# A filler tile in SBUF: the K and V buffers of a decode kernel begin at multiples of 512 bytes

## The chip, the cores and the metric

The kernel runs on one core of a Trainium2 chip. The metric is device time in microseconds (us); the kernel before takes 670.23 us, the median of three runs (670.22 to 670.27). TensorE is PE in the profile, VectorE is DVE, ScalarE is ACT, GpSimd is POOL and SyncE is SP. DMA transfers are issued by SP, and at the start by ACT, and carried out by 16 DMA engines.

## The reference

One decode step of a transformer block for four tokens (B = 4, width 512). A conditioning vector gives six modulation vectors. The first half is attention of one query per batch over a cache of 4096 keys and values in each of 32 heads of 128 elements; the second half is a small gated MLP.

```python
mod = (_silu(c) @ w_mod).reshape(c.shape[0], 6, 1, -1)
h = _layernorm(x, axis=-1) * (1 + ca) + sa
x = x + ga * _A_ref(h, A_k_cache, A_v_cache, A_wq, A_wo)   # attention over the cache
h = _layernorm(x, axis=-1) * (1 + cb) + sb
x = x + gb * _B_ref(h, B_w_in, B_w_sp, B_b_sp, B_w_out)    # gated MLP
```

Inside `_A_ref`: `q = x @ wq`, scores `q . k` for 4096 keys, softmax, the weighted sum of the values, and the projection by `wo`. All inputs are bf16. The two caches hold 4 x 32 x 4096 x 128 elements each, 134 MB each; all else is small beside them.

## The kernel before, in words

**Tiling.** The 128 (batch, head) pairs are treated four heads at a time: NQ = 32 rounds, round i being head group g = i // 4 of batch b = i % 4. A round needs 4 MiB of K and 4 MiB of V. A K tile lies as [128 partitions, 128 x 128 elements]: partition 32 h + s holds the 128 consecutive keys of slot s of head h, 32,768 consecutive bytes of the cache. V lies the same way. So each partition of a tile is one unbroken piece in HBM and one in SBUF.

**Buffers.** Two K tiles (kt0, kt1) and two V tiles (vt0, vt1), each 32,768 bytes a partition, are the first tiles of the SBUF pool `sb`; the pool hands out places in the order in which tiles are asked for. In front of them lie 16,384 bytes that the program keeps for DMA and four small constants, so kt0 begins at byte 16512 of each partition. Behind them come some 80 small tiles: the identity `ident`, the query `qbc` (8192 bytes), softmax vectors, weights. Before round 0 the V tiles serve as landing places for two weights, w_mod in vt0 and wq in vt1.

**A round.** SP issues the load of the next K tile and of this round's V tile (line 141, where every DMA is recorded). In some rounds a 512 KB piece of `wo` (tile wo_g) is loaded too. DVE multiplies half a K tile by the query in place (`scores`, recorded at line 136: kt<-kt,qbc, 8192 elements), and PE adds up the 128 products of each key by 16 matmuls with the identity (lines 355 and 360). DVE folds the partial sums (S<-bank), does the softmax's maximum by reductions and transposes (mx, mT, hm, hb, nm), ACT takes the exponential (E), and DVE spreads it over the four heads (P). PE multiplies the V tile of the round before by P (line 349, bank<-vt,P), and ACT copies the result out (osb).

**What sets the order.** `Program` records every operation, finds which one needs which by the regions of the tiles that they read and write, and gives each engine its operations in the order of the Python code, with semaphore waits. A K load waits until PE has finished with the tile that it overwrites, a V load until PE has finished the values of two rounds before. SP issues in that fixed order.

**The end.** The last K and V tiles are loaded in pieces, and behind them on the same queue come the last part of wo (wo_l), win and wout. A tail of small operations (projection, layer norm, gated MLP) follows, and a transfer of 4 KB brings the output to HBM.

The functions that allocate, as the diff touches them:

```python
    def tile2(shape, dtype, name, n=2):
        return [sb.tile(shape, dtype, name=f"{name}{a}") for a in range(n)]

    kt = tile2([P, NT * DH], BF16, "kt")
    vt = tile2([P, NT * DH], BF16, "vt")
```

Of the kernel before, what the change touches and what calls it, by code (L numbers as in the profile page):

```python
# [7 lines left out]
BF16 = mybir.dt.bfloat16  # L8
# [218 lines left out]
def kernel(  # L227
# [17 lines left out]
    P = 128  # L245
# [19 lines left out]
    sb = ctx.enter_context(tc.tile_pool(name="sb", bufs=1))  # L265
    pm = ctx.enter_context(tc.tile_pool(name="pm", bufs=1, space=bass.MemoryType.PSUM))

    def tile2(shape, dtype, name, n=2):
        return [sb.tile(shape, dtype, name=f"{name}{a}") for a in range(n)]

    kt = tile2([P, NT * DH], BF16, "kt")
    vt = tile2([P, NT * DH], BF16, "vt")
    rows = sb.tile([2 * B, D], BF16, name="rows")
# [500 lines left out]
```

## Time and profile before

| what | value |
|---|---|
| median of three runs | 670.23 us (670.22 to 670.27) |
| the profiled execution | 670.11 us |
| its span, first to last instruction | 668.3 us |
| DVE busy | 402.9 us, 60% of the span, 475 instructions |
| PE busy | 420.4 us, 63% |
| ACT busy | 41.3 us, 6% |
| bytes by DMA | 282.90 MB in 12673 packets, mean 423 GB/s |
| granted TensorE clock, mean | 0.772 |

How to read the views. The slices cut the span in 40 equal parts, each digit being the busy share of an engine in tenths. A row of a group of instructions names line, engine, operation, output<-inputs with their shapes, the count, then busy time and the mean ns of one, then the idle time of the engine just before them and what ended it. A row of DMA issues gives the count, the KB of one and the median us from issue to landing. A row of the table by windows gives the window, its length, then for each engine the busy us and (in brackets) the instructions, in the order PE, PEld (weight loads), DVE, ACT, POOL, then the granted clock, the DMA share and GB/s. A timeline row gives start, length, engine, line and operation; in square brackets stands the idle time before it and what ended it. A packet is one descriptor's piece of a transfer on one DMA engine.

### The profile page before, as it was taken

To read this page: it belongs to the slowest core of one execution; us is meant where nothing else is said; L and a number is where in the kernel's file an instruction comes from. 1 tells how busy PE (TensorE), PEld (TensorE's weight loads), DVE (VectorE), ACT (ScalarE), POOL (GpSimd) and SP (SyncE) were. 2 spreads that over 40 slices of the span, in tenths; PEclk is the share of its full clock that TensorE was granted. 3 is DMA by queue.
4 is the path that set the end of the run, shared out by engine and by line. 5 is a ranking of instruction groups with operands and counts; after the bars stand their busy time and mean duration, and the time that the engine had idled before them with its cause. 6 is when DMAs were issued, how large, how long until landed. Compare 5 with 4: busy or idle time off the path is not lost.

```text
span 668.3 us, 5909 instructions
## 1 busy us (share of the span) xinstructions
PE 420.4 (63%) x3024; PEld 94.2 (14%) x2065; DVE 402.9 (60%) x475; ACT 41.3 (6%) x115; POOL 3.2 (0%) x17
## 2 busy tenths in 40 slices
PE   2557776665576754576655667656557675557784
PEld 2201110011111101111001111101111110111124
DVE  2177766676456666555756654757655666655662
ACT  1200000000000000000000000000000000000002
POOL 1000000000000000000000000000000000000000
PEclk9988876767888767888766788766788876788885
DMA  9999999999999999999999999999999999999995
GB/s 377 430 426 430 436 430 430 429 437 426 431 431 437 430 426 431 435 430 426 435 435 430 430 431 435 430 428 431 437 428 430 431 437 426 431 431 437 422 410 198
DMA packets 12673, 282.90 MB, mean 423 GB/s; under 512 B 1388, under 2 KB 1908, under 8 KB 3956
## 3 DMA queue, kind: packets, MB, share of 16 engines
q1 hardware_dynamic: 12640, 282.73, 98.8%
q8 instruction: 7, 0.11, 0.1%
q14 instruction: 6, 0.05, 0.0%
q10 hardware_dynamic: 20, 0.01, 0.0%
HBM read 282.73 MB, written 0.00 MB: 423 GB/s over the span
## 4 chain that ended last, share of the span: by engine, by line
DMA 63%; PE 24%; DVE 12%; issue 0%; SPq 0%; ACT 0%; DVEq 0%
DMA kt<-in_A_k_cache_dram 58%; PE bank L360 23%; DVE kt L136 11%; DMA vt<-in_A_v_cache_dram 3%; DMA wout<-in_B_w_out_dram 1%; PE bank L349 0%; SPq L141 0%; DVE S L136 0%; DVE P L136 0%; ACT E L136 0%; DVE mx L136 0%; DVE nm L136 0%; DVE mT L136 0%; DVE hm L136 0%; DVE hb L136 0%
## 5 line engine op out<-in xcount | busy, mean ns | idle before, releaser
L360 PE MATMUL bank<-kt,ident 128*128 128x512 bf16 x1024 | 295.0, 459 | 180.9 <-DVE kt L136 180.9
L136 DVE TENSOR_TENSOR kt<-kt,qbc 128x8192 bf16<-128x8192 bf16 x64 | 282.7, 4420 | 86.6 <-DMA kt<-in_A_k_cache_dram 86.6
L136 DVE TENSOR_REDUCE S<-bank 128x64 f32<-128x512 f32 x64 | 44.3, 692 | 125.6 <-PE bank L360 125.6
L355 PEld LDWEIGHTS <-ident 128*128 128x128 bf16 x64 | 9.1, 142 | 359.4 <-issue 359.3
L349 PE MATMUL bank<-vt,P 128*32 128x512 bf16 x992 | 59.2, 380 | 0.5 <-DMA vt<-in_A_v_cache_dram 0.5
L349 PE MATMUL bank<-sel,osb 128*128 128x4 f32 x248 | 35.7, 267 | 29.4 <-ACT osb L136 25.0
L136 ACT ACTIVATE E<-S,nm 128x128 f32<-128x128 f32 x32 | 12.8, 401 | 568.3 <-DVE nm L136 568.3
L349 PEld LDWEIGHTS bank<-sel,osb 128*128 128x128 f32 x248 | 33.0, 207 | 41.9 <-ACT osb L136 36.9
L136 DVE TENSOR_TENSOR P<-E,mask 128x512 bf16<-128x512 f32 x32 | 22.2, 693 | 18.0 <-ACT E L136 18.0
L349 PEld LDWEIGHTS bank<-rs,ones_f 128*128 128x128 f32 x64 | 12.1, 190 | 104.8 <-issue 104.0
L349 PEld LDWEIGHTS bank<-vt,P 128*32 128x32 bf16 x992 | 23.6, 96 | 21.4 <-DMA vt<-in_A_v_cache_dram 0.6
L136 ACT COPY osb<-bank 128x512 f32<-128x512 f32 x31 | 17.5, 565 | 17.4 <-PE bank L349 17.3
L349 PE MATMUL bank<-vt,hbc 128*32 128x512 bf16 x128 | 8.9, 448 | 4.7 <-DMA vt<-in_A_wq_dram 4.7
L349 PE MATMUL bank<-oP,wo_g 128*128 128x4 bf16 x112 | 3.9, 165 | 10.2 <-DVE oP L136 10.2
L136 DVE RECIPROCAL rz<-bank 128x4 f32<-128x4 f32 x32 | 5.6, 176 | 7.3 <-PE bank L349 7.3
L136 DVE TENSOR_REDUCE mx<-S 128x1 f32<-128x128 f32 x32 | 9.2, 286 | 1.1
L349 PE MATMUL bank<-rs,ones_f 128*128 128x4 f32 x64 | 9.1, 212 | 0.0
L136 DVE STREAM_TRANSPOSE nm<-hb 128x32 f32<-128x32 f32 x32 | 6.8, 212 | 1.1
L136 DVE STREAM_TRANSPOSE mT<-mx 128x32 f32<-128x32 f32 x32 | 6.8, 212 | 1.1
L136 DVE TENSOR_SCALAR rs<-mask,rs 128x4 f32<-128x4 f32 x32 | 7.2, 224 | 0.0
L136 DVE TENSOR_REDUCE hm<-mT 128x1 f32<-128x32 f32 x32 | 6.0, 186 | 1.1
L136 DVE TENSOR_SCALAR hb<-hm 128x32 f32<-128x32 f32 x32 | 5.8, 181 | 1.1
(91 smaller groups left out, 75.5 us busy)
## 6 DMA issues: line engine op xcount, KB each, us to landing
kt<-in_A_k_cache_dram SPq DMA_DIRECT2D x31, 4096.0 KB, 25.8
vt<-in_A_v_cache_dram SPq DMA_DIRECT2D x31, 4096.0 KB, 33.1
vt<-in_A_wq_dram SPq DMA_DIRECT2D x1, 4096.0 KB, 20.5
kt<-in_A_k_cache_dram SPq DMA_DIRECT2D x2, 2048.0 KB, 24.7
wo_g<-in_A_wo_dram SPq DMA_DIRECT2D x7, 512.0 KB, 22.8
vt<-in_w_mod_dram SPq DMA_DIRECT2D x1, 3072.0 KB, 10.2
vt<-in_A_v_cache_dram SPq DMA_DIRECT2D x1, 2048.0 KB, 19.8
win<-in_B_w_in_dram SPq DMA_DIRECT2D x1, 1344.0 KB, 14.8
```

What stands on the lines that cost most here:

```text
L136: eng, lambda e: getattr(e, name)(*args, **kw), ins, outs, sem=sem, done=done, after=after,
L349: "PE", lambda e: e.matmul(out, lhsT=lhsT, rhs=rhs, start=start, stop=stop, **kw),
L355: prog.add("PE", lambda e: e.ldweights(lhsT), [lhsT], [], done=False)
L360: return e.add_instruction(mybir.InstMatmult(name=nc.get_next_instruction_name(), engine=mybir.EngineType.PE, ins=[e.lower_ap(rhs), e.lowe ...
```

## The change

One tile is asked for ahead of kt0, 192 bf16 elements (384 bytes) on each partition. Nothing reads or writes it. The tiles after it keep their order and sizes.

```diff
@@ -268,6 +268,8 @@
     def tile2(shape, dtype, name, n=2):
         return [sb.tile(shape, dtype, name=f"{name}{a}") for a in range(n)]
 
+
+    fill = sb.tile([P, 192], BF16, name="fill")
     kt = tile2([P, NT * DH], BF16, "kt")
     vt = tile2([P, NT * DH], BF16, "vt")
     rows = sb.tile([2 * B, D], BF16, name="rows")
```

## The prediction

> **What bounds the kernel now.** I read the page's slices first. The three rows are the busy share of DVE, the mean busy share of the 16 DMA engines, and the rate.
>
> ```profile
> DVE  2177766676456666555756654757655666655662
> ...
> DMA  9999999999999999999999999999999999999995
> GB/s 377 430 426 430 436 430 430 429 437 426 431 431 437 430 426 431 435 430 426 435 435 430 430 431 435 430 428 431 437 428 430 431 437 426 431 431 437 422 410 198
> ```
>
> The DMA digit is 9 up to the last slice, while DVE is near 6. The rate is flat at about 431 GB/s, so the stream of K and V has no hole. The DMA part of the page names the queue that carries it, with its packets, megabytes and share of 16 engines' span:
>
> ```profile
> q1 hardware_dynamic: 12640, 282.73, 98.8%
> ```
>
> Next the table by windows, cut at 40 us (loop running), 620, 650 and 663 us (last landing; I leave out the windows between). Its last two numbers are DMA share and GB/s.
>
> ```profile
> 2.00:10.00 8.00, 0.50 (x9) 0.44 (x9) 0.96 (x6) 1.47 (x2) 1.90 (x10) 1.00 1.01 399
> ...
> 40.00:620.00 580.00, 368.04 (x2394) 73.15 (x1502) 365.36 (x396) 28.45 (x89) 0.00 (x0) 0.76 1.00 431
> ...
> 650.00:663.00 13.00, 8.50 (x220) 7.81 (x220) 2.72 (x17) 2.87 (x6) 0.00 (x0) 0.51 0.80 302
> 663.00:668.30 5.30, 0.91 (x19) 0.54 (x16) 1.40 (x8) 1.11 (x3) 0.22 (x1) 0.50 0.00 1
> ```
>
> The share is 1.00 while K and V stream, 0.80 while the last weights come, and 0 after 663. The timeline of the end shows what starts the tail:
>
> ```profile
> 653.90 0.33 SPq L141 DMA_DIRECT2D wout<-in_B_w_out_dram  x1
> ...
> 663.33 0.49 PE L360 MATMUL bank<-u,wout 128*128 128x12 bf16 x12 [0.17 <-DMA wout<-in_B_w_out_dram]
> ```
>
> That weight load is issued as the last piece of V lands (653.88 in the chain of waits) and lands 9.38 us later, at 663.28; the matmuls that need it start at 663.32. So the time is a sum: 1.9 us until the first transfers, 652.0 us in which K and V stream, 9.4 us for the weights still queued, 5.0 us from the last landing to the end of the span (668.3), and 1.8 us around the span: 670.1, the profiled execution's 670.11. The median of the runs, 670.23, is 0.12 us above it.
>
> The check on the 652.0 are the trace's packet records, one for each descriptor, with start, duration and bytes: between 40 and 620 us the packets' durations add up to 1.00 of 16 engines' time, one packet behind the other. Only the price of a packet, or a hole in the stream, can move its end.
>
> **How much cover the engines have.** One K tile in the timeline (start, length, engine, line):
>
> ```profile
> 218.80 4.42 DVE L136 TENSOR_TENSOR kt<-kt,qbc 128x8192 bf16<-128x8192 bf16 x1 [3.12 <-DMA kt<-in_A_k_cache_dram]
> ...
> 223.28 8.93 PE L360 MATMUL bank<-kt,ident 128*128 128x512 bf16 x32 [4.48 <-DVE kt L136]
> ...
> 232.24 0.33 SPq L141 DMA_DIRECT2D kt<-in_A_k_cache_dram  x1
> ...
> 235.35 0.23 DVE L136 TENSOR_SCALAR rs<-mask,rs 128x4 f32<-128x4 f32 x1
> ...
> 238.25 4.43 DVE L136 TENSOR_TENSOR kt<-kt,qbc 128x8192 bf16<-128x8192 bf16 x1 [2.67 <-DMA kt<-in_A_k_cache_dram]
> ```
>
> A tile's work takes DVE from 218.80 to 235.58, 16.8 us of a period of 19.45, and then DVE waits 2.67 us for the next K. Over the kernel:
>
> ```profile
> L136 DVE TENSOR_TENSOR kt<-kt,qbc 128x8192 bf16<-128x8192 bf16 x64 | 282.7, 4420 | 86.6 <-DMA kt<-in_A_k_cache_dram 86.6
> ...
> kt<-in_A_k_cache_dram SPq DMA_DIRECT2D x31, 4096.0 KB, 25.8
> ```
>
> 86.6 us over 30 waits is 2.9 us of slack a tile. Below it, a K transfer lands 25.8 us after its issue. A whole transfer alone takes 8 packets on each engine, 8 x 1217 ns = 9.7 us, so some 16 us of older transfers still stand ahead of it when SP issues it. Those 16 us are the cover of everything ahead of SP's issue.
>
> **The change, part by part.**
>
> *The filler itself.* No instruction names it. The two programs have the same 1893 instructions in the same order with the same waits; no DMA is added, split or moved past another. Cost 0, hidden behind nothing.
>
> *The addresses.* In the two built layouts every one of the kernel's 81 tiles moves up by 384 bytes; kt0 goes from byte 16512 (128 over a multiple of 512) to 16896 (33 x 512), and the other three follow, since a tile is 64 x 512 bytes. 384 is 3 x 128: distances between tiles stay, and so does each start modulo 128. The change can act only through address bits 7 and 8 and above. In HBM nothing moves.
>
> *DMA packets.* Each partition of a K or V tile is one packet of 32,768 bytes. There are 8064 such packets (62 K and V transfers and wq, 128 each), 504 for each engine, and they run one behind the other. So 1 ns on such a packet is 504 x 1 ns = 0.50 us of the end. (The pieces of the last two tiles are another 896 packets, 56 for each engine; I leave this ninth out.) What can an aligned start save? The fastest packet of each size in the records, with its start in SBUF modulo 256: 32,768 bytes 1213 ns (128), 16,384 bytes 611 (128), 8,192 bytes 309 (128), 4,096 bytes 159 (wo_g, 224), 3,584 bytes 140 (win, 160), 3,072 bytes 121 (wout, 160), 2,048 bytes 84 (128). The first and the fourth give (1213 - 159) / 28,672 = 0.03676 ns a byte. What is left over on each is 8.4, 8.7, 7.9, 8.4, 8.3, 8.1 and 8.7 ns. Three different offsets, one remainder: the offset moves a packet by some 0.6 ns at most, 0.3 us in 504. But none of these starts at a multiple of 256, so the upper bound of the gain is the whole remainder: 504 x 8.4 ns = 4.2 us, 666.0. One row lies near: the output's packets leave SBUF from a multiple of 512. They have 256 bytes in 15 ns, a remainder of 5.6, or 2.8 less; 504 x 2.8 ns = 1.4 us. It is the other direction, and 1 ns is the records' resolution.
>
> The steady packets take 1217.5 ns in the mean, 4.5 over the fastest. That excess isn't a matter of place: wq goes to vt1, the same bytes as every odd V tile, and its 128 packets take 1213 in the median with no spread, while later V packets there take 1217. So it stays.
>
> For a loss the nearest row is that spread: the slowest twentieth of the steady packets takes 1222 ns, 4.5 over the mean; 504 x 4.5 = 2.3 us, 672.5. Between +2.3 and -4.2 I take the row nearest to the case, the three offsets with one remainder: 0, within 0.3 us.
>
> [...]
>
> *DVE and PE on the moved tiles.* DVE's 64 multiplies take 4412 to 4427 ns, PE's fastest matmul on kt 379 ns; no row has another alignment. I cost them at 0: the 2.9 us of DVE slack hide up to 1.45 us on each of a tile's two multiplies, a third of its length. With the cover gone, each ns is paid. Lower bound of their effect: 0 as well, since a faster multiply only waits longer for the same K.
>
> *The small tiles of the tail.* They lie outside DMA, 5.0 us in which DVE is busy 1.40 and PE 0.91. Their starts modulo 128 stay; 0.
>
> Sum: 670.11 + 0 = 670.1 for a profiled run, **670.2** for the median.
>
> **The rivals.** About 0.2% is what a measurement of this kernel can tell from no change: 1.34 us, or 2.7 ns on a packet.
>
> A. *Aligned rows make the packet cheaper.* For it: every packet of a K or V tile now starts and ends on a 512 boundary, and one row at such a boundary has 2.8 ns less. Against: one remainder at three offsets. Price 1.4 to 4.2 us; the middle is 2.8, so 667.4. Chance 0.16.
>
> B. *Packets become dearer*, because their first writes at new address bits meet engine accesses to SBUF. Place: queue q1, every packet. Price 4.5 ns a packet, so 672.5; it decides from 2.7 ns. Against: packets that run wholly beside a busy DVE take 1217.2 ns, those beside an idle one 1216.9. Chance 0.07.
>
> C. *The multiply leaves its pace* at the new place. 8192 elements in 4420 ns are 1.85 a ns; at half that a tile's chain grows by 8.8 us, 5.9 over the slack, and 31 tiles give 183 us: 853. It decides from 2.9 us a tile, when DVE takes the end from DMA. Against: all starts modulo 128 and all distances stay. Chance 0.02.
>
> D. *It doesn't do what it says.* A tile that nobody uses could take no space; the built layout shows it does. And the physical start of SBUF could lie off a multiple of 512. 670.2 again, chance 0.02.
>
> **How the numbers follow.** Forecast 0.73, A 0.16, B 0.07, C 0.02, D 0.02. Same is 0.73 + 0.02 = 0.75, faster 0.16, slower 0.09. The range goes from A's middle, 667.4, to B's price, 672.5; it leaves out half of A, C and a part of B, some 0.14. The forecast's own range is 668.9 to 671.5.
>
> **What will show it.** If I am right: 32,768-byte packets at 1213 at the least and 1217 in the mean, 431 GB/s between 40 and 620 us, multiplies at 4420 ns, some 87 us of waits of DVE for K. A: the fastest packet under 1211 and a higher rate. B: a mean over 1220 with the same fastest packet. C: multiplies over 5.9 us, DVE's waits for K gone and DMA digits under 9. A change of the time with the same packets would mean a hole in the stream that I have not seen, and would refute the whole sum.

## The result, and the profile after

The changed kernel takes **667.12 us** (median of 5 runs, 666.84 to 667.17) against 670.22 us of before on the same chip: ratio 0.9953, 95% interval 0.9939 to 0.9967. That is 3.1 us less, and 0.3 us under the low end of the range, which was the middle of rival A, 667.4. The profiled execution took 666.94 us, its span is 665.1.

The page's slices after, in the same rows as before (DVE, DMA, GB/s), and the queue that carries the stream:

```profile
DVE  2166777676556666555766655757655666655662
...
DMA  9999999999999999999999999999999999999995
GB/s 379 427 425 438 436 426 432 438 432 432 432 437 432 432 432 437 428 432 431 442 426 432 441 428 434 432 436 432 432 434 437 430 432 436 436 430 430 435 413 214
...
q1 hardware_dynamic: 12640, 282.73, 98.8%
```

The DMA digit is 9 in all slices but the last, as before, with the same packets and bytes. The GB/s are a little higher. The table by windows, of the kernel after, shows it for the running loop (last two numbers: DMA share and GB/s):

```profile
40.00:620.00 580.00, 363.79 (x2401) 71.31 (x1502) 367.81 (x396) 28.43 (x89) 0.00 (x0) 0.76 1.00 433
```

433 GB/s in place of 431, with the same DMA share of 1.00 and the same granted clock: no hole was filled; each busy nanosecond moved more. The engines do the same as before. From the groups and the DMA issues of the page after:

```profile
L136 DVE TENSOR_TENSOR kt<-kt,qbc 128x8192 bf16<-128x8192 bf16 x64 | 282.7, 4419 | 88.3 <-DMA kt<-in_A_k_cache_dram 88.2
...
kt<-in_A_k_cache_dram SPq DMA_DIRECT2D x31, 4096.0 KB, 25.8
```

The multiply takes 4419 ns (4420 before), and DVE's waits for K are 88.2 us (86.6). The chain of waits ends in the same steps, about 3 us earlier (start, length, what). Before:

```profile
631.49 22.39 DMA vt<-in_A_v_cache_dram
...
653.90 9.38 DMA wout<-in_B_w_out_dram
```

After:

```profile
629.34 21.41 DMA vt<-in_A_v_cache_dram
...
650.77 9.33 DMA wout<-in_B_w_out_dram
660.10 0.05 issue
660.14 0.50 PE bank L362 x12
```

The last piece of V lands at 650.75 in place of 653.88; from there the weights take 9.33 us (9.38) and the tail the rest. So nearly all of the gain stands in the stream of K and V, up to its last pieces.

**Where it sits in the stream.** The packet records say it. These are the packets of 32,768 bytes that start between 60 and 600 us (4 in some 7000 that last over 1300 ns, in either kernel, are left out):

| | fastest | mean | share over the fastest by more than 1 ns |
|---|---|---|---|
| before | 1213 ns | 1217.1 | 68% |
| after | 1213 ns | 1213.0 | 0% |

The fastest packet hasn't changed. The spread above it, 4.1 ns in the mean, is gone: all but 1 packet in 1000 take 1213. 504 x 4.1 ns = 2.1 us, and the stream's packet number 7680 starts 2.1 us earlier after (599.85 against 601.96 us). Another 0.8 us shows where the last whole tile comes in: its last packet ends 2.9 us earlier (641.76 against 644.66 us). The trace has 16 landing events for a tile, and DVE's multiply starts after the last of them; 0.5 of the 0.8 us stands there: for the K tile that lands at 576.10 us before (multiply at 576.13) and 573.44 after (573.46), the last event comes 2.60 us behind the median one before, 2.07 after. The short packets of the end give the last 0.2 us or so: the 1024-byte packets of wo_l take 46.0 ns in the mean after, 49.7 before, though they still begin off a multiple of 256 (96 bytes past one, 224 before).

### The profile page after: what moved, and what is told of

It is laid out like the page before. It is cut to its first block, busy times and chain, and to the rows that moved or that the text cites. A ratio compares the mean times of both kernels' runs of the same rounds, so it can differ in the third digit from the quotient of the medians.

```text
span 665.1 us, 5909 instructions
## 1 busy us (share of the span) xinstructions
PE 414.2 (62%) x3024; PEld 92.6 (14%) x2065; DVE 402.7 (61%) x475; ACT 41.2 (6%) x115; POOL 3.2 (0%) x17
## 4 chain that ended last, share of the span: by engine, by line
DMA 63%; PE 23%; DVE 12%; issue 0%; SPq 0%; ACT 0%; DVEq 0%
DMA kt<-in_A_k_cache_dram 58%; PE bank L362 23%; DVE kt L136 11%; DMA vt<-in_A_v_cache_dram 3%; DMA wout<-in_B_w_out_dram 1%; PE bank L351 0%; SPq L141 0%; DVE S L136 0%; DVE P L136 0%; ACT E L136 0%; DVE mx L136 0%; DVE nm L136 0%; DVE mT L136 0%; DVE hm L136 0%; DVE hb L136 0%
## 5 line engine op out<-in xcount | busy, mean ns | idle before, releaser
L362 PE MATMUL bank<-kt,ident 128*128 128x512 bf16 x1024 | 289.6, 453 | 183.5 <-DVE kt L136 183.5
L136 DVE TENSOR_TENSOR kt<-kt,qbc 128x8192 bf16<-128x8192 bf16 x64 | 282.7, 4419 | 88.3 <-DMA kt<-in_A_k_cache_dram 88.2
L351 PE MATMUL bank<-sel,osb 128*128 128x4 f32 x248 | 33.8, 260 | 29.3 <-ACT osb L136 24.9
L351 PEld LDWEIGHTS bank<-sel,osb 128*128 128x128 f32 x248 | 31.1, 197 | 41.8 <-ACT osb L136 36.8
```

Of the source, the lines that this page charges most:

```text
L136: eng, lambda e: getattr(e, name)(*args, **kw), ins, outs, sem=sem, done=done, after=after,
L351: "PE", lambda e: e.matmul(out, lhsT=lhsT, rhs=rhs, start=start, stop=stop, **kw),
L362: return e.add_instruction(mybir.InstMatmult(name=nc.get_next_instruction_name(), engine=mybir.EngineType.PE, ins=[e.lower_ap(rhs), e.lowe ...
```

## The experiments

The theory after the result: a packet of the stream has an extra of about 4 ns, paid in the DMA itself, while K and V begin off a multiple of 256 (or 512). Rivals: it is the small tiles' places; it is the shift as such; it comes from engines that use SBUF beside the writes; and later, which part of a packet makes it. Every run stands beside runs of the kernel before on the same chip (medians 670.25 to 670.38 us).

"Mean" below is that of the stream's packets as in the table above, "base" their fastest.

### Which place: four fillers

Run 1, a filler of 128 bytes:

```diff
+    fill_a = sb.tile([P, 64], BF16, name="fill_a")
     kt = tile2([P, NT * DH], BF16, "kt")
```

> A filler of 128 bytes: K and V tiles begin at 256 over a multiple of 512, every tile of the kernel moves by 128. Theory 256 (a packet's extra cost comes from a start off a multiple of 256): steady packets of 32,768 bytes flat at 1213 ns, about 667.1 us as with the filler of 384. Theory 512 (only multiples of 512 are free of it): packets at 1217 in the mean, about 670.2 us. Theory small tiles (it is where the small tiles lie, not K and V): anything, most likely not equal to either.

Measured: 667.13 us, ratio 0.9953 (0.9937 to 0.997); base 1213, mean 1213.0. A start at 256 over a multiple of 512 does all that the change does.

Run 2, a filler of 256 bytes (`[P, 128]` in the same place):

> A filler of 256 bytes: K and V tiles begin at 384 over a multiple of 512, 128 off a multiple of 256. Theories 256 and 512 both: packets at 1217 ns in the mean with a spread, 670.2 us. Theory 'any other place than the first helps': 1213 ns and about 667 us.

Measured: 670.34 us, ratio 1.0002 (0.9992 to 1.0011); mean 1217.1, 67% over the base. 128 off a multiple of 256 costs the same on both sides of it.

Run 3, a filler of 512 bytes (`[P, 256]`):

> A filler of 512 bytes: every start modulo 512 as before, all tiles moved. Theories 256 and 512: no change, 1217 ns and 670.2 us. Theory 'it is the shift as such, or bits above 8': faster than before by some us.

Measured: 670.22 us, ratio 0.9999 (0.999 to 1.0009); mean 1217.1. A shift as such does nothing. The running loop in the table by windows (runs 1, 2, 3 in this order):

```profile
40.00:620.00 580.00, 373.83 (x2400) 72.89 (x1502) 367.60 (x396) 28.43 (x89) 0.00 (x0) 0.76 1.00 433
```

```profile
40.00:620.00 580.00, 364.86 (x2396) 71.46 (x1502) 365.30 (x396) 28.43 (x89) 0.00 (x0) 0.76 1.00 431
```

```profile
40.00:620.00 580.00, 365.47 (x2394) 73.19 (x1502) 364.93 (x396) 28.46 (x89) 0.00 (x0) 0.76 1.00 431
```

The last number goes with the boundary: 433 at a multiple of 256, 431 off it. PE's busy time (373.83, 364.86, 365.47) doesn't go with it.

Run 4, the small tiles put back where they stood modulo 512:

```diff
+    fill_a = sb.tile([P, 192], BF16, name="fill_a")
     kt = tile2([P, NT * DH], BF16, "kt")
     vt = tile2([P, NT * DH], BF16, "vt")
+    fill_c = sb.tile([P, 64], BF16, name="fill_c")
```

> 384 bytes ahead of K and V and 128 bytes behind them: K and V begin at multiples of 512, all small tiles stand modulo 512 where they stood before. Theories 256 and 512 (K and V starts alone): 1213 ns and 667.1 us. Theory small tiles: 670.2 us. The packets of wo_g, then again 224 off a multiple of 256, tell whether a packet pays for its own start (4096 bytes at 162 to 163 ns in the mean) or for its neighbours' (159 to 160).

Measured: 667.35 us, ratio 0.9956 (0.9939 to 0.9973); mean 1213.0. K and V alone matter. And wo_g's packets, 224 off a multiple of 256 as before the change, take 159.6 ns in the mean (162.8 before), nearly the fastest, 159: **a short transfer off the boundary amid an aligned stream pays 0.6 ns in place of 3.8.** A packet doesn't simply pay for its own start.

### K or V alone

Run 5 (`fill` of 384 bytes ahead of kt, 128 bytes between kt and vt) and run 6 (384 bytes between kt and vt only):

> 384 bytes ahead of K and 128 bytes between K and V: K tiles begin at multiples of 512, V tiles at 128 over one, as before. Theory own start (a packet pays for its own start off a multiple of 256): K packets 1213 ns, V packets 1217, half of the gain, about 668.7 us. Theory stream (misaligned packets disturb the packets that other engines move beside them, or leave the engines in a phase that lasts): K packets above 1213 too, or V packets at 1213, and a time away from 668.7.

> 384 bytes between K and V: K tiles at 128 over a multiple of 512 as before, V tiles at multiples of 512. Theory own start: V packets 1213 ns, K packets 1217, about 668.7 us, the mirror of the run with K alone. Theory stream: the two kinds don't part so.

Measured: 668.31 us with K aligned, 0.9971 (0.9959 to 0.9982), and 668.16 us with V, 0.9969 (0.9956 to 0.9981). Either half gives about two thirds of the gain. The packets don't part as "own start" wants: with K aligned, K packets take 1213.4 and V packets 1214.2; with V aligned, 1213.5 and 1213.6. (The records name no tile; the two kinds are told apart by their order in the stream, 128 packets to a transfer.) Over both kinds the extra falls to a fifth with K aligned (0.8 ns) and to a seventh with V aligned (0.55). It isn't a fixed price of a misaligned packet. It grows while such packets follow each other. In the kernel before, the mean is 1213.0 from 10 to 22 us, 1213.4 from 22 to 40, 1214.5 from 40 to 55 and 1217.1 from 55 us on; with K aligned it creeps from 1213.3 (55 to 100 us) to 1214.0 (300 to 400) and stays there (1213.9 from 400 to 620).

Two more places in the same records bear on this. With K aligned, the seven V transfers right behind a load of wo_g, which lies off the boundary too, pay 3.3 ns in the mean, the other V transfers 0.5: most of V's extra stands where two misaligned transfers follow each other. And in the kernel after, win and wout lie 32 bytes past a multiple of 256. The 3584-byte packets of win begin flat behind the aligned stream, at 140 ns for the first quarter of them from 649.5 us on; 4 us later they pay 4 to 5 ns. In run 12 below, where they lie on the boundary, they stay flat to the end. So the build-up doesn't belong to the start of the program, and its length isn't fixed: some 45 us there, 4 us here.

### Engines or DMA alone

Runs 7 and 8 leave out most of the work on K and V, without and with the 384 bytes in front:

```diff
-            "tensor_tensor", out=kh, in0=kh,
-            in1=qbc[:, b, g, :][:, None, :].to_broadcast([P, HT, DH]), op=MULT, sem="pe_dve",
+            "tensor_tensor", out=kh[:, 0:1, :], in0=kh[:, 0:1, :],
+            in1=qbc[:, b, g, :][:, None, :], op=MULT, sem="pe_dve",
...
-        n = DH // DC
+        n = 1
...
-        NU = NT // 16
+        NU = 1
```

> The kernel before with nearly all work on K and V left out: DVE multiplies 128 of the 8192 elements of a half tile, PE does one matmul of its 16, and 4 of the 32 on V; all loads and waits stay. Theory engines (the extra comes from engine accesses to SBUF beside the writes): packets flat at 1213 ns, and the same time as the next run. Theory DMA alone (it comes from the DMA engines among themselves): 1217 ns as in the kernel before, 3 us more than the next run, both within a few us of 670 and 667 since DMA sets the end.

> The same left out, with the 384 bytes in front (starts at multiples of 512). Both theories: packets flat at 1213 ns. The time against the run before this one decides: equal for theory engines, 3 us less for theory DMA alone.

Measured: 670.35 us without, 1.0001 (0.9991 to 1.0011), and 667.33 us with the filler, 0.9956 (0.9939 to 0.9972). The running loop in the table by windows, run 7, then run 8:

```profile
40.00:620.00 580.00, 113.83 (x692) 83.00 (x691) 113.39 (x388) 31.31 (x87) 0.00 (x0) 0.50 1.00 431
```

```profile
40.00:620.00 580.00, 113.80 (x692) 82.95 (x691) 113.37 (x388) 31.31 (x87) 0.00 (x0) 0.50 1.00 433
```

The group of the multiply on run 7's page:

```profile
L136 DVE TENSOR_TENSOR kt<-kt,qbc 128x128 bf16<-128x128 bf16 x64 | 14.0, 221 | 429.2 <-DMA kt<-in_A_k_cache_dram 429.2
```

DVE's multiplies are 14.0 us busy (282.7 before) and wait 429 us for K, and the time is still 670.35. That shows twice over that DMA sets the end, and that the extra (mean 1217.2) doesn't come from the engines' accesses to K and V: with the filler the same idle kernel has 1213.0.

### What in a packet

Runs 9 and 10 load each K and V row without its first 128 bytes, in the layout of before (run 9) and of the change (run 10):

```diff
-            load_sp(..., kt[i % 2][:, a:b], kv_view(A_k_cache, i)[:, a:b])
+            load_sp(..., kt[i % 2][:, max(a, 64):b], kv_view(A_k_cache, i)[:, max(a, 64):b])
```

The same for V; the first 64 elements of kt are zeroed once by POOL.

> The layout of before (tiles at 128 over a multiple of 512), but every K and V row is loaded without its first 128 bytes: 32,640 bytes from 128 past a multiple of 256 in HBM to a multiple of 256 in SBUF. The first 64 elements of each row are left out. A packet without extra is 1213 - 128 x 0.03676 = 1208.3 ns, and the whole 2.3 us shorter than with full rows. Theory destination (the write's start alone counts): flat at 1208 ns, 667.1 - 2.3 = 664.8 us. Theory difference (source and destination must agree modulo 256): packets with a spread, some 1212 ns, 667.9 us or more.

> The same rows without their first 128 bytes in the changed layout: 128 past a multiple of 256 in HBM to 128 past one in SBUF. Theory destination: packets with a spread, some 1212 ns in the mean, 670.2 - 2.3 = 667.9 us. Theory difference: flat at 1208 ns, 664.8 us.

Measured: 666.49 us (0.9944, 0.9928 to 0.9959) and 666.25 us (0.9939, 0.9923 to 0.9954). The base is 1208 in both, as worked out; the mean is 1209.6 and 1209.7, 27% of the packets over the base. Both theories fall. Neither an aligned write nor equal offsets make the packets flat, and the extra is 1.6 ns in both, less than half of 4.1.

Run 11, a filler of 160 bytes (`[P, 80]`), K and V 32 bytes past a multiple of 256:

> A filler of 160 bytes: K and V begin 32 bytes past a multiple of 256. Theory 256 (any start off a multiple of 256 pays): 1217 ns with a spread, 670.2 us. If the amount matters: something between, or more than with 128 off.

Measured: 670.72 us, 1.0006 (0.9997 to 1.0015); mean 1217.9, 94% over the base by more than 1 ns. 32 bytes off are at least as bad as 128.

Runs 13 and 14 drop the last 128 bytes of each row in place of the first, in the layout of the change (13) and of before (14), `a:min(b, NT * DH - 64)`; the last 64 elements of kt0, kt1 and vt0 are zeroed once by POOL:

> The layout of the change; each K and V row without its last 128 bytes (64 elements of each row are left out): 32,640 bytes that begin at a multiple of 256 in HBM and in SBUF and end 128 past one. A packet without extra is 1208 ns. Theory start (a packet pays when it begins off a multiple of 256 at either side): flat at 1208, 667.1 - 2.3 = 664.8 us. Theory pieces (it pays for a broken piece of 256 bytes at either of its ends): some 1209.5 ns and 666.3 us, as without the first 128 bytes.

> The layout of before; each row without its last 128 bytes: begins at a multiple of 256 in HBM, 128 past one in SBUF, where it ends at a multiple of 256. Theory start: as before the change, 4 ns of extra, 1212 ns and 670.2 - 2.3 = 667.9 us. Theory pieces: 1209.5 ns and 666.3 us.

Measured: 666.05 us (0.9937, 0.992 to 0.9953) and 666.66 us (0.9944, 0.9928 to 0.9961); means 1209.6 and 1209.7 over a base of 1208. "Start" falls: an aligned start on both sides with a ragged end pays 1.6 ns, and a write that starts off but ends on a boundary pays no more. "Pieces" fits the packets, though not as a count: each of these four kernels breaks one 256-byte piece on the HBM side (counted from the start of the cache) and one on the SBUF side of a packet, and the kernel before, which breaks two on the SBUF side (first and last), pays 4.1. But in all four the length isn't a multiple of 256 either, which these runs don't tell apart; and 504 x 1.6 ns on 664.8 us give 665.6, so 0.4 to 1.1 us of these times isn't accounted for.

Runs 15 and 16 load each tile as two halves, each with a semaphore of its own, in the layout of before and with the 128-byte filler:

```diff
-        for n, part in enumerate((2, 2) if i == NQ - 1 else (1,)):
+        for n, part in enumerate((2, 2)):
...
-        for n, part in enumerate((2, 4, 8, 16, 16) if i == NQ - 1 else (1,)):
+        for n, part in enumerate((2, 4, 8, 16, 16) if i == NQ - 1 else (2, 2)):
```

> The layout of before, every K and V tile loaded as two halves of 16,384 bytes a partition: twice the packets, each with the fixed remainder of 8.4 ns, 504 x 8.4 = 4.2 us more. Theory per packet (the extra is paid once by each packet): 504 x 4 ns more on top, 677 us, and 3 x 2 = 6 us over the next run. Theory per byte: 674.4 us, 3 us over the next run. The shorter packets of the last tiles, 4 ns over the fastest at 8192 bytes as at 32,768, speak for per packet.

> The same halves with the filler of 128 bytes, starts at multiples of 256: packets flat at 611 ns, 667.1 + 4.2 = 671.3 us by all theories. If the remainder of 8.4 ns is not paid in a row but hidden between packets: 667 us.

Measured: 675.15 us (1.0071, 1.0054 to 1.0088) and 670.00 us (0.9994, 0.9985 to 1.0004), 5.15 us apart. Packets of 16,384 bytes take 614.7 off the boundary and 611.0 on it, an extra of 3.7 ns on half the bytes. So it is paid by the packet, not by the byte. 1008 x 3.7 ns are 3.7 us of the 5.15; as with whole rows, a part of the time doesn't stand in the mean packet. The 504 packets more on each engine cost 670.00 - 667.13 = 2.9 us, 5.7 ns each: less than the remainder of 8.4. Packets overlap by an estimated 3 ns: in the kernel after, a whole transfer lands 9.68 us after the one before it, 8 x 1210 ns, where a packet's record lasts 1213.

The table by windows of run 15, then of run 16:

```profile
40.00:620.00 580.00, 364.85 (x2372) 71.35 (x1500) 366.25 (x393) 30.09 (x89) 0.00 (x0) 0.76 1.01 428
```

```profile
40.00:620.00 580.00, 369.98 (x2382) 72.52 (x1500) 370.02 (x394) 29.81 (x89) 0.00 (x0) 0.76 1.01 431
```

Halving the packets costs 2 to 3 GB/s in either layout, and the boundary 3 (428 against 431), where it costs 2 with whole rows.

### Everything on the boundary

Run 12 puts wo_g, wo_l, win and wout at multiples of 256 as well:

```diff
+    fill_a = sb.tile([P, 64], BF16, name="fill_a")
     kt = tile2([P, NT * DH], BF16, "kt")
...
+    fill_b = sb.tile([P, 80], BF16, name="fill_b")
     wo_g = sb.tile([P, NH, D], BF16, name="wo_g")
...
+    fill_c = sb.tile([P, 32], BF16, name="fill_c")
     win = [sb.tile([P, j1 - j0, F], BF16, name=f"win{a}") for a, (j0, j1) in enumerate(WJS)]
```

> 128 bytes ahead of K and V, 160 ahead of wo_g and 64 ahead of win: K, V, wo_g, wo_l, win and wout all begin at multiples of 256. Theory 256 with the stream's memory: the weights' packets at the end, 3584 bytes at 143 ns and 3072 at 125 with the filler of 384, come down to 140 and 121; that is (32 x 3.2 + 8 x 3.8) ns on each engine, 0.13 us: 667.0 us, at the edge of what can be told from 667.1.

Measured: 666.99 us, 0.995 (0.9937 to 0.9964). The weights' packets became flat (3072 bytes at 121.0, 3584 at 140.0 but for a few long ones; 124.8 and 142.2 after the change), and that is worth an estimated 0.1 us, as expected: too little to be told from 667.12 and 667.13.

## Why the prediction was wrong

**What held.** DMA sets the end: with most of the engines' work left out it stays where it was (670.35 and 667.33 us in runs 7 and 8), and what moved it was the price of a packet, without a hole. Filler, instruction order, multiplies, matmuls and tail cost 0; 1 ns on a 32 KB packet is 0.5 us (2.1 us of the stream for 4.1 ns). Rivals B and C didn't come. D, no effect, is refuted by the result, and runs 1 to 3 show that the boundary is real.

**The step that failed** is this sentence: "That excess isn't a matter of place: wq goes to vt1, the same bytes as every odd V tile, and its 128 packets take 1213 in the median with no spread, while later V packets there take 1217. So it stays." The rows were right and the reading wrong. wq is the second transfer of the program, from 10 to 20 us, and the extra takes until 55 us to build up (1213.0, 1213.4, 1214.5, 1217.1). A sample from the start can't clear a cause that builds up. The packets of the same place, early and late, proved that place alone isn't enough, not that place has no part.

**The test of offsets** was of the wrong statistic. Three offsets with one remainder is true of the fastest packets: they are the ones that paid nothing, off or on the boundary (1213 in both kernels). The offset acts on the mean, and the mean of every size was in the same records: 8192-byte packets 4.4 ns over their fastest, 3072-byte ones 2.3, 2048-byte ones 3.0, 1024-byte ones 3.7. An extra that doesn't grow over a factor of 32 in size was the sign of a price by the packet that is not in the floor. Besides, all three offsets were off the boundary, as the prediction said, so they couldn't show the step at it.

**Rival A** had the direction, and not the mechanism: it took the gain from the remainder of 8.4 ns, which stayed, and put "the fastest packet under 1211" as its sign, which didn't come. That its middle, 667.4, lies 0.3 us from the result is luck. The term that was mis-sized is the spread: 4.5 ns costed at no gain, where 4.1 of it went (the rest is mostly the few packets over 1300 ns, which stayed). And 504 x 4.1 = 2.1 us is not all: DVE waits for the last of a tile's 16 landing events (0.5 us, as read at one K tile), and the tail's small packets pay too, 1.0 us that no term of the sum held. That took the result out of the range.

The boundary that the runs show for writes to SBUF is 256 bytes, not the 512 of the change (1213.0 ns in the mean in run 1, 1217.1 in run 2). In SBUF the fastest packet is 1213 ns on and off the boundary, and 32 bytes off (1217.9 in run 11) are no cheaper than 128. In HBM the reads of runs 9 and 10 begin 128 bytes past a multiple of 256 (counted from the start of the cache), and their fastest packets take 1208 ns like those of runs 13 and 14, whose reads begin on the boundary.

**What stays open.** Shown: K and V at multiples of 256 in SBUF, in packets of 32,768 and 16,384 bytes, have no extra (means of 1213.0 and 611.0 ns); off it they have about 4 ns by the packet (1217.1 and 614.7), with most of the engines' work left out too (1217.2 in run 7), after a run of such packets. Not shown: why it needs the run, and what sets the run's length.

## What to carry to other kernels

Where DMA sets the end, look at the records of its packets, not only at the share and the rate. Here the mean stood above the fastest of the same size by a few ns that didn't grow with size (4.1 at 32,768 bytes, 3.7 at 1024): a price by the packet, not by the byte (runs 15 and 16). It went when the big tiles began at multiples of 256 bytes in SBUF (1217.1 to 1213.0 ns), at the price of a filler of 128 bytes, and aligning one of two streams gave two thirds of the gain in time. And a sample from the first microseconds said nothing on an extra that took until 55 us to build up.

## What the runs showed of the hardware that was not expected

- A packet's extra depends on what went before it: 0.6 ns for wo_g, 224 off the boundary, amid aligned K and V; 0.5 ns for V packets off it between aligned K packets, but 3.3 where a misaligned load of wo_g comes just ahead; 4.1 ns when all are off.
- Aligned, the stream is exact: in the kernel after, the 7000 packets of 32,768 bytes between 60 and 600 us show 1213 ns from the 5th to the 95th in a hundred.
- Rows that break one 256-byte piece on the HBM side and one on the SBUF side pay 1.6 ns, whether the break is at the first or the last 128 bytes (runs 9, 10, 13 and 14: means of 1209.6 and 1209.7 over 1208).
- Cutting every transfer in half costs 5.7 ns for each added packet, 2.9 us in all (670.00 us in run 16, 667.13 in run 1), about as much as the alignment gives (3.1).
